# A two-layer feed-forward behind an attention: its instructions ordered by the list scheduler, in token groups of 768 instead of 576

## The chip, the cores and the metric

The kernel runs on one core of one Trainium2 chip. The metric is the device time of one execution in microseconds. Engines are named as in the profile: PE (TensorE; PEld is its weight load), DVE (VectorE), ACT (ScalarE), POOL (GpSimd), SP (SyncE, which issues nearly all DMAs).

## The reference

```python
def _attn_ref(q, k, v, f):              # (4, 8, 576, 64) each, f without the last axis
    scores = np.matmul(q, k.transpose(0, 1, 3, 2)) / sqrt(D)
    cum = np.cumsum(np.log(np.clip(f, 0.0001, 1.0)), axis=-1)
    scores = np.where(causal, -1e9, scores + cum[..., :, None] - cum[..., None, :])
    attn = softmax(scores)              # rows, with 1e-9 added to the sum
    return np.matmul(attn, v)
def _moe_ref(x, w_in, w_out):           # 2304 tokens, 512 -> 2048 -> 512
    h = x @ w_in
    return (h / (1 + np.exp(-h))) @ w_out
def _moe2_ref(x, w_a, w_b, w_out):      # 512 -> 1536 -> 512
    return (x @ w_a * (x @ w_b)) @ w_out
# x = attention, heads side by side, as (2304, 512); then _moe_ref, then _moe2_ref
```

The weights of both layers arrive as 64-bit floats and are turned into 32-bit ones on the chip. Every 32-bit operand of a feed-forward product is split into a high and a low part; three matmuls (high by high, high by low, low by high) make one product.

## The kernel before

**Attention** works on 16 pairs of heads. Its operations are recorded in `Plan` with a planned duration, a priority and the data and buffers that they need; `Plan.order` is a list scheduler that always takes the operation that can start first on some engine, the priority deciding between near equals. The result is emitted in that order, so each engine's queue has the planned order, and an engine waits whenever the next instruction in its queue is not ready.

**Feed-forward, first half of a layer** (`stage_in`). One `job(stage, u, b)` makes 256 output columns (unit u) for 576 tokens (batch b) with seven products instead of eight: inputs and weights are first combined and split into seven "forms" each (`make_forms`, `load_unit`), each product is six matmuls of 288 columns (line 731), and the results are put together and passed through the gate by ACT (copies, tanh) and DVE. Layer 0 has 8 units, layer 1 has 12, each for 4 batches: 80 jobs. Results go to DRAM (`gdram`, `cdram`). Two jobs run in step.

**Second half** (`stage_out`). Five blocks of tokens (four of 512, one of 256). For each of 16 (layer 0) or 12 (layer 1) steps f, a tile `gg` is loaded, ACT rounds it (`gh`, line 829), POOL takes the rest (`gl`, line 830), and PE runs 12 matmuls (line 835) into four banks of PSUM, which are read out at the block's end. gg, gh and gl share one pool of nine tiles with tag u, and so do the tiles that carry the result out (`evict_end`).

**Weights** are decoded in pieces of 128x512 (`decode`): one load of 512 KB (`raw`), one ACT operation, four of DVE (lines 627, 628, 630, 631) and one of POOL (632). A unit takes two pieces and then combinations and splits; the second matrix of layer 0 takes 16 pieces, that of layer 1 takes 12, each with a rounding on ACT and a difference on POOL (`load_out`, 794, 795). raw, m, e and v have one buffer each.

After the attention the order is that of the written code, rearranged by the tile framework's own scheduler; the engine of each operation is fixed in the code. In the order listings names end in numbers: `a0_6_2` is PSUM tile a of the job of layer 0, unit 6, batch or group 2; `gl0_512_3` belongs to layer 0, block at token 512, step 3.

## Time and profile before

| what | value |
| --- | --- |
| median of two runs | 1200.35 us (1198.18 to 1202.52) |
| the profiled execution | 1200.18 us |
| its span in the trace | 1198.5 us, so 1.7 us lie around it |
| PE busy | 1041.8 us, 87% of the span |
| DVE, POOL, ACT busy | 593.7, 584.6, 498.9 us |
| mean granted TensorE clock | 0.951 |

Busy times are sums over a profiled execution. A matmul counts as busy from its issue to its modelled end, so overlapping matmuls hide how closely they follow each other; the distance between their starts is read from the timeline. A DVE or POOL instruction counts as busy also while it is held up after its start.

### The profile page before, as it was taken

How to read it: one execution, taken by the hardware profiler on the slowest of the kernel's cores; microseconds unless marked ns; L12 is line 12 of the kernel's file. 1: busy time of each engine (PE TensorE's matmuls, PEld its weight loads, DVE VectorE, ACT ScalarE, POOL GpSimd, SP SyncE). 2: the span in 40 equal slices, each digit the busy share in tenths (PEclk: the TensorE clock that was granted, in tenths of full speed). 3: DMA queues.
4: the chain of work that ended last, by engine and by line, in shares of the span. 5: the costliest groups of instructions: out<-in, count | busy, mean ns of one | idle time of the engine just before them, and what ended most of it. 6: DMA issues, size and time to landing. Idle time of an engine off the chain costs nothing.

```text
span 1198.5 us, 18236 instructions
## 1 busy us (share of the span) xinstructions
PE 1041.8 (87%) x6656; PEld 892.8 (74%) x6656; DVE 593.7 (50%) x1218; ACT 498.9 (42%) x1141; POOL 584.6 (49%) x494
## 2 busy tenths in 40 slices
PE   8978999589899976885797998999999997788897
PEld 7646667489899854664565898998999995476686
DVE  6777765675786744446322016467565565300000
ACT  6786877445554542335123233233333233222212
POOL 5676620445452356679745452364543335543332
PEclk9998999889999989898798999999999998988898
DMA  5543331123343454342332211132322224333323
GB/s 151 167 131 122 116 109 43 50 80 132 133 162 124 147 178 128 118 149 71 102 100 78 77 49 41 50 121 93 112 93 96 95 96 150 127 106 106 110 71 106
DMA packets 60025, 128.54 MB, mean 107 GB/s; under 512 B 9884, under 2 KB 14124, under 8 KB 59904
## 3 DMA queue, kind: packets, MB, share of 16 engines
q1 hardware_dynamic: 59824, 126.94, 32.9%
...
q10 hardware_dynamic: 112, 0.45, 0.2%
q14 instruction: 37, 0.30, 0.1%
...
## 4 chain that ended last, share of the span: by engine, by line
PE 52%; DVE 17%; DMA 14%; ACT 6%; POOL 5%; issue 4%; SPq 1%; ACTq 0%; DVEq 0%; POOLq 0%
PE o L835 18%; PE a L731 13%; DMA raw<-in_w 10%; PE b L731 6%; PE g L731 4%; PE s L428 3%; PE pv L548 3%; DVE e L631 3%; DVE e L630 2%; DVE m L628 2%; DMA gg<-gdram 2%; ACT m L626 2%; PE t_y L504 2%; DVE t L574 2%; DVE m L627 2%
## 5 line engine op out<-in xcount | busy, mean ns | idle before, releaser
L835 PE MATMUL o<-gh,wo 128*128 128x512 f32 (+1 forms) x1120 | 348.2, 394 | 71.0 <-ACT gh L829 61.6
L835 PEld LDWEIGHTS o<-gh,wo 128*128 128x128 f32 x1120 | 215.2, 201 | 123.6 <-ACT gh L829 70.2
L731 PE MATMUL a<-x,whi 128*128 128x288 f32 x1280 | 267.8, 300 | 32.1 <-ACT c L741 20.5
L830 POOL TENSOR_TENSOR gl<-gg,gh 128x512 fp32r<-128x512 f32 (+1 forms) x140 | 171.3, 1229 | 176.1 <-ACT gh L829 143.7
L731 PEld LDWEIGHTS a<-x,whi 128*128 128x128 f32 x1280 | 207.0, 190 | 37.9 <-ACT c L741 21.2
L835 PE MATMUL o<-gl,wo 128*128 128x512 f32 (+1 forms) x560 | 217.7, 397 | 19.7 <-POOL gl L830 19.5
L731 PE MATMUL a<-x,wlo 128*128 128x288 f32 x640 | 189.9, 297 | 0.0
L829 ACT CAST gh<-gg 128x512 fp32r<-128x512 f32 (+1 forms) x140 | 80.3, 578 | 203.7 <-DMA gg<-gdram 90.7
L574 POOL TENSOR_TENSOR wlo<-v,whi 128x512 fp32r<-128x512 f32 (+2 forms) x60 | 93.1, 1558 | 129.5 <-ACT whi L650 121.0
L835 PEld LDWEIGHTS o<-gl,wo 128*128 128x128 f32 x560 | 112.5, 201 | 52.9 <-POOL gl L830 31.9
L632 POOL TENSOR_TENSOR v<-m,e 128x512 f32<-128x512 f32 x68 | 91.8, 1350 | 110.1 <-DVE e L631 106.0
L731 PE MATMUL b<-x,whi 128*128 128x288 f32 x640 | 135.1, 300 | 4.7 <-DVE c L756 3.5
L627 DVE TENSOR_SCALAR m<-m 128x512 uint32<-128x512 uint32 x68 | 37.2, 548 | 173.9 <-ACT m L626 169.4
L731 PEld LDWEIGHTS a<-x,wlo 128*128 128x128 f32 x640 | 121.2, 190 | 0.0
L731 PEld LDWEIGHTS b<-x,whi 128*128 128x128 f32 x640 | 103.7, 190 | 7.8 <-DVE c L756 4.6
L731 PE MATMUL b<-x,wlo 128*128 128x288 f32 x320 | 94.9, 297 | 0.0
L626 ACT ACTIVATE m<-raw 128x512 f32<-128x512 f32 x68 | 45.5, 669 | 102.4 <-DMA raw<-in_w 78.4
L756 DVE TENSOR_TENSOR c<-b,c 128x288 f32<-128x288 f32 x80 | 36.2, 455 | 91.8 <-ACT c L755 90.9
L860 DVE COPY out<-o 128x512 f32<-128x512 f32 (+1 forms) x10 | 6.3, 637 | 148.6 <-PE o L835 148.5
L380 POOL TENSOR_TENSOR qkl<-qk,qkh 128x304 fp32r<-128x304 f32 x60 | 49.7, 860 | 58.9 <-DVE qkh L376 42.9
L462 ACT ACTIVATE p<-p,nm 128x512 f32<-128x512 f32 (+3 forms) x128 | 70.7, 554 | 7.4 <-DVE nm L454 7.3
L731 PE MATMUL g<-x,whi 128*128 128x288 f32 x320 | 67.3, 298 | 4.3 <-DVE c L745 2.6
...
## 6 DMA issues: line engine op xcount, KB each, us to landing
...
```

Of the source, the lines that this page charges most:

```text
L380: plan.add("POOL", t_pool(QK // 4), lambda c=c: nc.gpsimd.tensor_sub(lo()[:, c], raw()[:, c], hi().bitcast(F32)[:, c]), [(hi, "h"), raw], ...
L428: nc.tensor.matmul(out, stat, b[:, k0 + j0:k0 + j0 + nj], start=step == 0, stop=step == 3)
L462: plan.add("ACT", t_act(sum(IB[ib]), 279), lambda b=b, c=c, nj=sum(IB[ib]): nc.scalar.activation(b()[:, :nj], b()[:, :nj], AF.Exp, bias=nm ...
L574: emit(eng, d, lambda: getattr(e, op)(*[a() for a in args]), reads, writes, prio)
L626: emit("ACT", t_act(n, 93), lambda: nc.scalar.activation(m(), high().bitcast(F32), AF.Copy, scale=2.0 ** -112), [raw], [m], pr)
L627: emit("DVE", t_dve(n, True), lambda: nc.vector.tensor_scalar(u(m), u(m), 3, None, ALU.logical_shift_left), (), [m], pr)
L632: emit("POOL", t_pool(n), lambda: nc.gpsimd.tensor_add(dst(), m(), e()), [m, e], [dkey], pr)
L731: nc.tensor.matmul(ps[:, :HB], a, m, start=start and k == 0 and i == 0, stop=k == 1 and i == 2, skip_group_check=not start)
L756: nc.vector.tensor_add(c2[:, 1], be[:, :HB], c2[:, 1])
L829: nc.scalar.copy(hi, g)
L830: nc.gpsimd.tensor_sub(lo, g, hi.bitcast(F32))
L835: nc.tensor.matmul(ps[oc][:, :n], a, m, start=f == 0 and i == 0, stop=f == nf - 1 and i == 2)
```

## The change

The feed-forward is recorded in the same `Plan` as the attention, and all of it is ordered by the list scheduler. Token groups are 3 of 768 instead of 4 of 576, so a product has 384 columns, and there are 60 jobs instead of 80. Jobs start one after another, each seven products behind the last, so that two overlap. Where an operation names two engines (`pool_dve`, `gate`) the scheduler picks one for each instruction. raw, m and e get two buffers; `v` is gone (the sum is written back into e). The tiles gg become a ring of seven in the place of a weight unit, gh and gl one tile `hl` with three buffers, which the jobs' tile `c` shares (tag u); attention output, job output, result tiles and some raw pieces share the four buffers of tag z. The unit loads lie at other places, and the two halves of a second matrix are loaded from the end of the first half into block 0. Below, "+" is the new code; the old functions stand above.

```diff
-HB = S // 2
-NU = 9
+GT, NG = 768, NT // 768
+HB = GT // 2
...
-    SLOTS = dict(qkh=2, qkl=2, dt=2, qkr=2, vt=2, th=4, t3=1, t4=1, s=4, t=2, pv=1, mm=1, z=2, u=NU, raw=1, m=1, e=1, v=1)
+    SLOTS = dict(qkh=2, qkl=2, dt=2, qkr=2, vt=2, th=4, t3=1, t4=1, s=4, t=2, pv=1, mm=1, z=4, u=3, raw=2, m=2, e=2)
+    SLOTS.update({k: 1 for k in ("wA", "wB", "wC", "X0", "X1", "X2")})
...
+    def pool_dve(n, fn, reads, writes, prio):
+        plan.add("POOL", 240 + 2.2 * n, lambda: fn(nc.gpsimd), reads, writes, prio,
+                 also=[("DVE", 160 + n / 0.7, lambda: fn(nc.vector))])
...
+    def gate(t, h, reads, writes, prio, pool_only=False):
+        def on_pool():
+            nc.gpsimd.tensor_mul(t(), t(), h())
+            nc.gpsimd.tensor_add(t(), t(), h())
+        ways = [("DVE", 160 + HB / 0.7, lambda: nc.vector.scalar_tensor_tensor(t(), t(), 1.0, h(), ALU.add, ALU.mult)),
+                ("POOL", 480 + 4.4 * HB, on_pool)]
+        first, *others = ways[1:] if pool_only else ways
+        plan.add(*first, reads, writes, prio, also=others)
...
+    def split(n, hi, lo, val, reads, key, pr):
+        act(n, lambda: nc.scalar.copy(hi(), val()), reads, [key + (0,)], pr)
+        pool_dve(n, lambda e: e.tensor_sub(lo(), val(), hi().bitcast(F32)), list(reads) + [key + (0,)], [key + (1,)], pr)
...
+    def make_forms(stage, g, slot, pr):
...
+        x = buf(None, f"X{slot}", [P, FORMS, 2, 2, HB], F32R, f"x_{stage}_{g}")
...
+        keys = [(z[n // 2], "q", n) for n in range(4)]
+        src = ins[stage, g] + (["late"] if stage == 0 and slot else [])
+        def combine(o, a, b, add):
+            pool_dve(2 * HB, lambda e: (e.tensor_add if add else e.tensor_sub)(quads[o](), quads[a](), quads[b]()),
+                     src + [keys[a], keys[b]], [keys[o]], pr)
...
+        def form(f, n):
+            split(2 * HB, lambda: x()[:, f, 0], lambda: x()[:, f, 1], quads[n], src + [keys[n]], (x, f), pr)
...
+    def decode(piece, after, pr, spare=False):
...
+        raw = buf(zp if spare else dcp, "z" if spare else "raw", [P, 2 * n], F32, f"raw_{piece}")
+        m, e = (buf(dcp, t, [P, n], F32, f"{t}_{piece}") for t in "me")
...
+        plan.dma(480, 8 * P * n, lambda: nc.sync.dma_start(u(raw), src.bitcast(U32)), after, [raw], pr)
...
+        pool(n, lambda g: g.tensor_add(e(), m(), e()), [m], ek, pr)
+        return e
...
+    def job(stage, u, g, t):
...
+        yield at(0)
+        a = bank("a" + name)
+        c = buf(up, "u", [P, 3, HB], F32, "c" + name)
+        pa, pc = (lambda: a()[:, :HB]), (lambda i: c()[:, i])
+        prod(a, 1, 0, True)
+        act(HB, lambda: nc.scalar.copy(pc(0), pa()), [a], [(c, 0)], at(0) - 3)
...
+        act(HB, lambda: nc.scalar.copy(pc(2), pb()), [b], [(c, 2)], at(1) - 3)
...
+        prod(a, 6, 2, False)
+        act(HB, lambda: nc.scalar.copy(pc(1), pa()), [a], [(c, 1)], at(2) - 3)
...
+        dve(HB, lambda e: e.tensor_add(pc(1), pb(), pc(1)), [b], [(c, 1)], at(3) - 3)
...
+        dve(HB, lambda e: e.tensor_add(pc(2), pa(), pc(2)), [a], [(c, 2)], at(4) - 3)
...
+        z = buf(zp, "z", [P, 2, 2, HB] if stage == 0 else [P, 2, HB], F32, "z" + name)
+        prod(gm, 2, 5, True)
+        dve(HB, lambda e: e.tensor_add(pc(0), pg(), pc(0)), [gm], [(c, 0)], at(5) - 3)
+        last = at(6) - 2
+        if stage == 0:
+            act(HB, lambda: nc.scalar.activation(z()[:, 1, 1], pc(2), AF.Tanh, scale=0.5), [(c, 2)], [(z, 3)], last)
+            dve(HB, lambda e: e.scalar_tensor_tensor(z()[:, 1, 1], z()[:, 1, 1], 1.0, pc(2), ALU.add, ALU.mult), [(c, 2)], [(z, 3)], last, True)
+            act(2 * HB, lambda: nc.scalar.activation(z()[:, 0], c()[:, 0:2], AF.Tanh, scale=0.5), [(c, 0), (c, 1)], [(z, 0), (z, 1)], last)
+            for i in range(2):
+                gate(lambda i=i: z()[:, 0, i], lambda i=i: pc(i), [(c, i)], [(z, i)], last, i == 0 and u > 2)
+            plan.dma(480, 4 * P * GT, lambda: nc.sync.dma_start(rows(gdram, 2 * u), z()[:, 0].rearrange("p h c -> p (h c)")),
+                     [(z, 0), (z, 1)], [("g", 0, 2 * u, g)], last)
...
+        else:
+            pool_dve(HB, lambda e: e.tensor_mul(z()[:, 1], pc(1), pc(2)), [(c, 1), (c, 2)], [(z, 1)], last)
+        yield at(6)
+        prod(a, 4, 6, False)
+        if stage == 0:
+            act(HB, lambda: nc.scalar.activation(z()[:, 1, 0], pa(), AF.Tanh, scale=0.5), [a], [(z, 2)], last)
+            dve(HB, lambda e: e.scalar_tensor_tensor(z()[:, 1, 0], z()[:, 1, 0], 1.0, pa(), ALU.add, ALU.mult), [a], [(z, 2)], last)
...
+    def load_out(stage, h, slot, pr):
+        nf = (F1, F2)[stage] // 2
+        t = wouts[stage, h] = buf(None, f"X{slot}", [P, nf, 2, DM], F32R, f"wo_{stage}_{h}")
+        for f in range(nf):
+            after = yield
+            p = pr + f * T_OUT[512] / 1000
+            m = decode(piece_of(stage, "out") + h * nf + f, after, p, h == 1)
+            split(PIECE, lambda f=f: t()[:, f, 0], lambda f=f: t()[:, f, 1], lambda m=m: m(), [(m, 0), (m, 1)], (t, f), p)
+        yield
...
+    def out_block(stage, t0, n, ring, t, evict, then=None):
...
+        ps = [bank(f"o{stage}_{t0}_{oc}") for oc in range(KC)]
...
+            i = next(turns[stage])
...
+            loaded = plan.dma(480, 4 * P * n, lambda f=f, g=g: nc.sync.dma_start(g(), src[f, :, t0:t0 + n]),
+                     [("g", stage, f, k) for k in range(t0 // GT, (t0 + n - 1) // GT + 1)], [(ring, i)], p - 14)
+            if then and AHEAD <= f < AHEAD + nf // 2:
+                then.send([loaded])
+            hl = buf(up, "u", [P, 2, n], F32R, f"hl{stage}_{t0}_{f}")
+            act(n, lambda hl=hl, g=g: nc.scalar.copy(hl()[:, 0], g()), [(ring, i)], [(hl, 0)], p - 6)
+            pool_dve(n, lambda e, hl=hl, g=g: e.tensor_sub(hl()[:, 1], g(), hl()[:, 0].bitcast(F32)), [(hl, 0), (ring, i)], [(hl, 1)], p - 6)
...
+            plan.add("PE", T_OUT[n], mms, [(hl, 0), (hl, 1), (wt, fi, 0), (wt, fi, 1)], ps, p)
+        evict(t0, n, ps, 1000 + t + nf * T_OUT[n] / 1000)
...
+        if pair == 7:
+            make_forms(0, 0, 0, 2 * pair + 3)
+        if pair in (3, 6, 10):
+            load_unit(0, (3, 6, 10).index(pair), 2 * pair + PRIO["dec"], [(heads[2 * pair + 1]['s1'], "h")])
...
+    late = plan.add("SP", 0, open_late, (), ["late"])
+    late.deps = {o for o in plan.ops if any(b.tag in att_tags for b in o.bufs)}
...
+    make_forms(0, 1, 1, 1000 + t - 5)
+    make_forms(0, 2, 2, 1000 + t - 2)
+    seq = by((0, 1, 2)) + each((3, 4)) + by((5, 6, 7))
...
+    hooks = {(u - 3, 2): [U(0, u, place(u, 0) - 20)] for u in range(3, U1)}
+    hooks[7, 1] = [lambda p=1000 + end(0) - 10: [g.send(()) for g in (begun(load_out(0, 0, 0, p)),) for _ in range(F1 // 2)]]
+    late_half = lambda p=1000 + end(F1 // 2) - 14: begun(load_out(0, 1, 1, p))
+    t = stage_in(0, U1, seq, hooks, t)
+    ring = buf(None, "wC", [P, 7, 512], F32, "ring0")
+    for n, (t0, nb) in enumerate(BLOCKS):
+        t += out_block(0, t0, nb, ring, t, evict_mid, None if n else late_half())
+        if n == 1:
+            make_forms(1, 0, 2, 1080 + t)
+            load_unit(1, 0, 1000 + t)
+        if n == 2:
+            load_unit(1, 1, 1000 + t)
...
+    seq = by((0, 1)) + each(range(2, 9)) + by((9, 10, 11))
...
+    hooks[11, 1] = [lambda p=1000 + end(0) - 10: [g.send(()) for g in (begun(load_out(1, 0, 2, p)),) for _ in range(F2 // 2)]]
+    late_half = lambda p=1000 + end(F2 // 2) - 14: begun(load_out(1, 1, 0, p))
+    t = stage_in(1, U2, seq, hooks, t)
+    ring = buf(None, "wA", [P, 7, 512], F32, "ring1")
+    for t0, nb in BLOCKS:
+        t += out_block(1, t0, nb, ring, t, evict_end, None if t0 else late_half())
...
+    order = keep_warm(plan.order())
...
-    stage_in(0, U1, (0, 1), lambda: rest([heads["xf", b]() for b in (2, 3)], (2, 3)), lambda: None)
-    stage_out(0, evict_mid)
-    stage_in(1, U2, (2, 3), lambda: rest([ys[2], ys[3]], (0, 1)), lambda: None)
-    stage_out(1, evict_end)
```

Where the order moves, at three places. First PE at the end of the attention (`pv_15` is the last pair's product with v). Before:

```order
L548 MATMUL pv_15_1_3090<-th_15_0_3035,vt_15_2885 64x448 x2
L548 MATMUL pv_15_1_3090<-th_15_1_3050,vt_15_2885 64x448 x2
L731 MATMUL b0_1_1_3339<-x1_15_298,whi_0_1_102 128x288 x2
L731 MATMUL b0_1_1_3339<-x1_15_298,wlo_0_1_103 128x288
L731 MATMUL b0_1_1_3339<-x1_15_298,whi_0_1_102 128x288 x2
L731 MATMUL b0_1_1_3339<-x1_15_298,wlo_0_1_103 128x288
L548 MATMUL pv_15_1_3090<-th_15_2_3054,vt_15_2885 64x320 x2
L548 MATMUL pv_15_1_3090<-th_15_3_3063,vt_15_2885 64x192 x2
```

After:

```order
L696 MATMUL a0_0_0_3034<-x_0_0_1838,w_0_0_793 128x384 x6
L558 MATMUL pv_15_1_3169<-th_15_0_3085,vt_15_2936 64x448 x2
L558 MATMUL pv_15_1_3169<-th_15_1_3099,vt_15_2936 64x448 x2
L558 MATMUL pv_15_1_3169<-th_15_2_3109,vt_15_2936 64x320 x2
L558 MATMUL pv_15_1_3169<-th_15_3_3127,vt_15_2936 64x192 x2
L558 MATMUL pv_15_1_3169<-th_15_4_3125,vt_15_2936 64x64 x2
L558 MATMUL pv_15_0_3180<-th_15_2_3109,vt_15_2936 64x128 x2
L696 MATMUL b0_1_0_3184<-x_0_0_1838,w_0_1_1328 128x384 x6
L696 MATMUL g0_0_0_3202<-x_0_0_1838,w_0_0_793 128x384 x6
L696 MATMUL a0_1_0_3143<-x_0_0_1838,w_0_1_1328 128x384 x6
L696 MATMUL a0_0_0_3034<-x_0_0_1838,w_0_0_793 128x384 x6
```

One product of 288 columns cut the last attention products in two; now they stand in one piece, with whole products of 384 columns ahead of them and behind. Of the changed kernel's feed-forward products, seven are ahead of `pv_15_1`.

Then POOL in block 0 of layer 0's second half, with the decode of its matrix (`v` or `e` the decoded piece, `wo` the split one). Before:

```order
L830 TENSOR_TENSOR gl0_0_0_5588<-gg0_0_0_5586,gh0_0_0_5587 128x512
L830 TENSOR_TENSOR gl0_0_1_5606<-gg0_0_1_5604,gh0_0_1_5605 128x512
L632 TENSOR_TENSOR v_8_84_5073<-m_8_86_5075,e_8_87_5076 128x512
L830 TENSOR_TENSOR gl0_0_2_5624<-gg0_0_2_5622,gh0_0_2_5623 128x512
L795 TENSOR_TENSOR wo_0_0_4994<-v_8_84_5073,wo_0_0_4994 128x512
L830 TENSOR_TENSOR gl0_0_3_5642<-gg0_0_3_5640,gh0_0_3_5641 128x512
L632 TENSOR_TENSOR v_8_88_5086<-m_8_90_5088,e_8_91_5089 128x512
L830 TENSOR_TENSOR gl0_0_4_5660<-gg0_0_4_5658,gh0_0_4_5659 128x512
L795 TENSOR_TENSOR wo_0_0_4994<-v_8_88_5086,wo_0_0_4994 128x512
L830 TENSOR_TENSOR gl0_0_5_5678<-gg0_0_5_5676,gh0_0_5_5677 128x512
```

After:

```order
L795 TENSOR_TENSOR hl0_0_2_4936<-ring0_4777,hl0_0_2_4936 128x512
L795 TENSOR_TENSOR hl0_0_4_4949<-ring0_4777,hl0_0_4_4949 128x512
L651 TENSOR_TENSOR e_22_4932<-m_22_4794,e_22_4932 128x512
L651 TENSOR_TENSOR e_23_4971<-m_23_4930,e_23_4971 128x512
L604 TENSOR_TENSOR wo_0_0_4518<-e_23_4971,wo_0_0_4518 128x512
L795 TENSOR_TENSOR hl0_0_6_5019<-ring0_4777,hl0_0_6_5019 128x512
L795 TENSOR_TENSOR hl0_0_7_5040<-ring0_4777,hl0_0_7_5040 128x512
L651 TENSOR_TENSOR e_24_5024<-m_24_4998,e_24_5024 128x512
L651 TENSOR_TENSOR e_25_5046<-m_25_5002,e_25_5046 128x512
L604 TENSOR_TENSOR wo_0_1_5071<-e_25_5046,wo_0_1_5071 128x512
```

The differences for the block's steps, all on POOL before, are spread: steps 2, 4, 6 and 7 are here, steps 0, 1, 3 and 5 are on DVE. DVE at the same place, before:

```order
L627 TENSOR_SCALAR m_8_90_5088<-m_8_90_5088 128x512
L628 SCALAR_TENSOR_TENSOR m_8_90_5088<-raw_8_89_5087,m_8_90_5088 128x512
L630 TENSOR_SCALAR e_8_91_5089<-m_8_90_5088 128x512
L631 SCALAR_TENSOR_TENSOR e_8_91_5089<-raw_8_89_5087,e_8_91_5089 128x512
L627 TENSOR_SCALAR m_8_94_5228<-m_8_94_5228 128x512
L628 SCALAR_TENSOR_TENSOR m_8_94_5228<-raw_8_93_5227,m_8_94_5228 128x512
L630 TENSOR_SCALAR e_8_95_5229<-m_8_94_5228 128x512
L631 SCALAR_TENSOR_TENSOR e_8_95_5229<-raw_8_93_5227,e_8_95_5229 128x512
```

After:

```order
L604 TENSOR_TENSOR wo_0_0_4518<-e_21_4804,wo_0_0_4518 128x512
L743 TENSOR_TENSOR c0_7_2_4806<-g0_7_2_4875,c0_7_2_4806 128x384
L795 TENSOR_TENSOR hl0_0_1_4908<-ring0_4777,hl0_0_1_4908 128x512
L747 SCALAR_TENSOR_TENSOR z0_7_2_4905<-z0_7_2_4905,c0_7_2_4806 128x384
L596 SCALAR_TENSOR_TENSOR z0_7_2_4905<-z0_7_2_4905,c0_7_2_4806 128x384
L649 TENSOR_SCALAR e_22_4932<-m_22_4794 128x512
L646 TENSOR_SCALAR m_23_4930<-m_23_4930 128x512
L650 SCALAR_TENSOR_TENSOR e_22_4932<-raw_22_4750,e_22_4932 128x512
L647 SCALAR_TENSOR_TENSOR m_23_4930<-raw_23_4860,m_23_4930 128x512
L795 TENSOR_TENSOR hl0_0_3_4945<-ring0_4777,hl0_0_3_4945 128x512
L759 SCALAR_TENSOR_TENSOR z0_7_2_4905<-z0_7_2_4905,a0_7_2_4783 128x384
L649 TENSOR_SCALAR e_23_4971<-m_23_4930 128x512
```

DVE had the decode alone; now gates, the last evictions of jobs, splits of `wo` and steps of `hl` stand between its parts.

Third, ACT at the border of blocks 0 and 1 in the second half of layer 1 (`out` carries the result). Before:

```order
L829 CAST gh1_0_10_10645<-gg1_0_10_10644 128x512
L829 CAST gh1_0_11_10663<-gg1_0_11_10662 128x512
L794 CAST wo_1_1_10153<-v_20_256_10219 128x512
L862 COPY out_0_0_10680<-o1_0_0_10460 128x512
L862 COPY out_0_2_10686<-o1_0_2_10462 128x512
L829 CAST gh1_512_0_10697<-gg1_512_0_10696 128x512
L829 CAST gh1_512_1_10715<-gg1_512_1_10714 128x512
L829 CAST gh1_512_2_10733<-gg1_512_2_10732 128x512
L829 CAST gh1_512_3_10751<-gg1_512_3_10750 128x512
```

After:

```order
L794 CAST hl1_0_11_9118<-ring1_8794 128x512
L603 CAST wo_1_1_8985<-e_66_9081 128x512
L794 CAST hl1_512_0_9128<-ring1_8794 128x512
L603 CAST wo_1_1_8985<-e_67_9123 128x512
L794 CAST hl1_512_1_9163<-ring1_8794 128x512
L794 CAST hl1_512_2_9191<-ring1_8794 128x512
L826 COPY out_0_1_9195<-o1_0_1_8870 128x512
L826 COPY out_0_2_9199<-o1_0_2_8874 128x512
L826 COPY out_0_3_9202<-o1_0_3_8878 128x512
L794 CAST hl1_512_3_9206<-ring1_8794 128x512
```

The roundings for three steps of the next block now stand ahead of the copies of the old block's result.

## Rows read from the trace of the kernel before

**Rows 1.** Page, part 1: engine, busy us (share of the span), instructions.
```profile
...
PE 1041.8 (87%) x6656; PEld 892.8 (74%) x6656; DVE 593.7 (50%) x1218; ACT 498.9 (42%) x1141; POOL 584.6 (49%) x494
...
```

**Rows 2.** Windows, one row per stage: width, then engines, TensorE clock, DMA share, GB/s.
```profile
...
0.00:218.00 218.00, 195.12 (x1684) 141.16 (x1684) 146.89 (x492) 162.71 (x446) 107.57 (x114) 0.98 0.38 117
218.00:503.00 285.00, 234.31 (x1470) 212.22 (x1468) 181.14 (x300) 129.79 (x274) 141.61 (x107) 0.93 0.39 129
503.00:713.00 210.00, 174.09 (x794) 139.31 (x793) 64.38 (x57) 65.85 (x131) 129.98 (x104) 0.92 0.30 92
713.00:993.00 280.00, 269.21 (x1987) 266.31 (x1986) 173.55 (x331) 92.53 (x210) 115.28 (x96) 0.99 0.26 87
993.00:1198.50 205.50, 169.04 (x729) 133.79 (x727) 27.77 (x40) 47.98 (x83) 90.12 (x74) 0.91 0.36 111
...
```

**Rows 3.** Waits of PE: us in total, times, longest.
```profile
...
PE o L835 <- ACT gh L829: 61.6, 19, 11.7
...
PE o L835 <- POOL gl L830: 19.5, 24, 3.3
...
```

**Rows 4.** Timeline of PE, 402 to 404 us: start, us, engine, line.
```profile
...
402.33 0.42 PE L731 MATMUL g<-x,whi 128*128 128x288 f32 x2
...
403.93 0.42 PE L731 MATMUL g<-x,whi 128*128 128x288 f32 x2
...
```

**Rows 5.** Timeline of PE, 679 to 684 us.
```profile
...
679.71 0.62 PE L835 MATMUL o<-gh,wo 128*128 128x512 f32 x2
...
683.91 0.39 PE L835 MATMUL o<-gh,wo 128*128 128x512 f32 x1
```

**Rows 6.** Timeline of PE at the end of the span.
```profile
...
1193.72 0.28 PE L835 MATMUL o<-gl,wo 128*128 128x256 f32 x1
...
1194.32 0.28 PE L835 MATMUL o<-gh,wo 128*128 128x256 f32 x1
```

**Rows 7.** Windows of line 731 alone on PE, attention.
```profile
...
0.00:218.00 218.00, 12.97 (x84) 0.98 0.38 117
...
```

**Rows 8.** Timeline of DVE, 332 to 335 us.
```profile
...
332.11 2.50 DVE L775 SCALAR_TENSOR_TENSOR t<-t,c 128x576 f32<-128x576 f32 x2
334.54 0.81 DVE L745 TENSOR_TENSOR c<-g,c 128x288 f32<-128x288 f32 x2
```

**Rows 9.** Timeline of POOL, 332 to 335 us.
```profile
...
332.27 1.73 POOL L632 TENSOR_TENSOR v<-m,e 128x512 f32<-128x512 f32 x1 [0.63 <-DVE e L631]
334.52 0.73 POOL L574 TENSOR_TENSOR wlo<-v,whi 128x256 fp32r<-128x256 f32 x1 [0.52 <-ACT whi L650]
```

**Rows 10.** Single lines: ns min/median/max, first and last start, forms.
```profile
L627 DVE TENSOR_SCALAR m<-m x68: 410/428/1641, 31.8 to 1037.0; 128x512 uint32<-128x512 uint32 x68
...
L778 DVE TENSOR_TENSOR t<-c,c x48: 443/459/1583, 722.5 to 994.8; 128x288 f32<-128x288 f32 x48
...
L775 DVE SCALAR_TENSOR_TENSOR t<-t,c x32: 743/756/1955, 232.1 to 428.0; 128x576 f32<-128x576 f32 x32
...
L756 DVE TENSOR_TENSOR c<-b,c x80: 444/458/460, 221.5 to 991.6; 128x288 f32<-128x288 f32 x80
...
L632 POOL TENSOR_TENSOR v<-m,e x68: 1260/1289/2312, 35.1 to 1040.4; 128x512 f32<-128x512 f32 x68
...
L574 POOL TENSOR_TENSOR v<-v x80: 722/742/1252, 56.5 to 934.5; 128x256 f32<-128x256 f32 x80
```

**Rows 11.** Groups of DVE and POOL, 435 to 495 us: busy us, mean ns, idle before.
```profile
...
L630 DVE TENSOR_SCALAR e<-m 128x512 uint32<-128x512 uint32 x7 | 8.8, 1259 | 0.2
...
L830 POOL TENSOR_TENSOR gl<-gg,gh 128x512 fp32r<-128x512 f32 x16 | 22.6, 1410 | 11.7 <-ACT gh L829 11.7
...
L632 POOL TENSOR_TENSOR v<-m,e 128x512 f32<-128x512 f32 x8 | 10.2, 1279 | 8.8 <-DVE e L631 8.8
```

**Rows 12.** Waits of SP and of ACT, 1000 to 1198 us.
```profile
...
SPq L828 <- PE o L835: 65.0, 26, 3.6
...
ACT gh L829 <- DMA gg<-cdram: 89.2, 39, 5.4
...
```

More of the change, by code (lines that the diff above doesn't have):

```diff
@@ L110, in add @@
         op.mode = mode
+        op.deps.update(k for k in reads if isinstance(k, Op))
+        reads = [k for k in reads if not isinstance(k, Op)]
         for k in list(reads) + list(writes):
@@ L315, in prepare, with group @@
                  ["dec"], pr, eng="ACT")
-    heads = {}
+    heads, groups, ins = {}, {}, {}
+    def group(stage, g):
+        if (stage, g) not in groups:
+            groups[stage, g] = [buf(zp, "z", [P, 2, GT], F32, f"z{r}_{stage}_{g}") for r in range(2)]
+        return groups[stage, g]
     decays = [sb.tile([P, 2 * S + P], BF16, name=f"decay{n}") for n in range(SLOTS["dt"])]
@@ new lines, in model_kernel, with product, mms @@
+    PROD = {1: (0, 0), 2: (1, 1), 3: (4, 2), 4: (2, 6), 5: (6, 3), 6: (3, 4), 7: (5, 5)}
+    xs, units, same, wouts = {}, {}, {}, {}
+    T_PROD = 6 * (HB / 2.4 + 13.5)
+    def product(ps, stage, u, g, n, start, pr):
+        wt, x = units[stage, u], xs[stage, g]
+        fw, fx = PROD[n]
+        def mms():
+            for k in range(2):
+                wh, wl = (wt()[:, i, fw, k * P:(k + 1) * P] for i in range(2))
+                xh, xl = (x()[:, fx, i, k] for i in range(2))
+                for i, (a, b) in enumerate(((wh, xh), (wh, xl), (wl, xh))):
+                    nc.tensor.matmul(ps()[:, :HB], a, b, start=start and k == 0 and i == 0, stop=k == 1 and i == 2,
+                                     skip_group_check=not start)
+        key = (wt, same.get((wt, fw), fw))
+        plan.add("PE", T_PROD, mms, [key + (i,) for i in range(2)] + [(x, fx, i) for i in range(2)], [ps], pr)
@@ new lines, in evict_end @@
+    def evict_end(t0, n, ps, p):
+        for oc in range(KC):
+            o = buf(zp, "z", [P, n], F32, f"out_{t0}_{oc}")
+            reads, writes = [ps[oc]], [o]
+            plan.add("ACT", 190 + n / 1.2, lambda o=o, oc=oc: nc.scalar.copy(o(), ps[oc]()[:, :n]), reads, writes, p,
+                     also=[("DVE", 160 + n / 0.96, lambda o=o, oc=oc: nc.vector.tensor_copy(o(), ps[oc]()[:, :n]))])
+            plan.dma(480, 4 * P * n, lambda o=o, oc=oc: nc.sync.dma_start(out[oc * P:(oc + 1) * P, t0:t0 + n], o()), [o], [("out", t0, oc)], p)
@@ L691, in model_kernel @@
         attend(pair)
-        if pair in (3, 7):
-            b = pair // 4
-            make_forms(planned, b, heads["xf", b], heads["xf", b], 2 * pair + 3, ("POOL", ["POOL", "DVE"] * 3 + ["POOL"]))
-        if pair in (2, 5):
-            load_unit(planned, 0, len(units), 2 * pair + PRIO["dec"], [(heads[2 * pair + 1]['s1'], "h")])
-    turn = cycle(BANKS)
-    def later(name):
-        tag = next(turn)
-        return (mm if tag == "mm" else aps).tile([P, 512], F32, name=name, tag=tag, bufs=SLOTS[tag])
+        if pair == 7:
+            make_forms(0, 0, 0, 2 * pair + 3)
@@ L709, in model_kernel @@
         temp.close()
[L710 to L712 removed]
+        open_big()
         for op in order[split:]:
             op.fn()
[L715 to L721 removed]
```

406 lines of the change are left out of this document (166 added, 240 removed).

## The prediction

> **What bounds the kernel now.** PE is busy for 87% of the span [rows 1], so I first ask how much of that is needed. The timeline gives the distance of matmuls that follow each other without a gap: 12 of 288 columns start from 402.33 to 403.93, 0.1333 us each [rows 4]; 18 of 512 from 679.71 to 683.91, 0.2333 each [rows 5]; of 256 columns 0.12 each [rows 6]. The code has 80 jobs of 42 matmuls, 3360 x 0.1333 = 448 us, and 28 steps f in each of the five blocks, 28 x (48 x 0.2333 + 12 x 0.12) = 354 us. Together the feed-forward needs 802 us of PE. The attention ends at 218 us, 84 feed-forward matmuls (11 us) already done [rows 7]; the remaining 791 us of work take the 980 us to the end. So about 190 us are lost after the attention, and the stages show where [rows 2]. The first half of layer 0 with block 0 (218 to 503) needs 1260 x 0.1333 + 16 x 2.80 = 213 us and takes 285: 72 lost. The other blocks (503 to 713) need 157 and 4 us of early jobs and take 210: about 50 lost. The first half of layer 1 takes 280 for 264: 16 lost. Its second half needs 152 and takes 205.5: some 50 lost, 4 of them behind the last matmul [rows 6].
>
> The waits of PE name ACT's rounding and POOL's difference in the blocks [rows 3]. Behind them stand two causes. In the blocks of layer 1, SP waits 65 us for PE before it may issue the next tile's load, and ACT then waits 89 us for those loads [rows 12]: nine tiles of tag u give three steps of lead, and the result tiles take from the same nine. From 435 to 495, where the matrix is decoded, the cause is another. Two additions of DVE that read PSUM run beside POOL and take 0.81 us together, but two instructions of line 775 that read two tiles from SBUF take 2.50 us against a smallest 0.743 each, just as POOL's line 632 takes 1.73 against 1.26 [rows 8 to 10]. DVE's work on two SBUF tiles, and its fast one-input operations (line 627: 0.41 at best, 1.64 at worst), take turns with POOL; line 756, which reads PSUM, never grows (444 to 460 ns) [rows 10]. Added up at the smallest durations, POOL's 32 instructions from 435 to 495 (16 of line 830, 8 each of 632 and 795) are 40.3 us, and DVE's four decode lines (14 at 0.41, 15 at 0.68) 15.9: 56 of 60 us, 94% [rows 11]. I call this turn-taking the shared port. So block 0 of layer 0 is bound by the port, the later blocks by the depth of buffers, the first halves nearly by PE.
>
> The Trainium skill (SBUF — State Buffer, "SBUF: two separate sides") speaks against planning DVE and POOL side by side: the port pair that the two share is an exclusive lock held for a whole instruction, taken by GpSimd and by DVE operations in a two-port mode or with two SBUF inputs. By that rule, the trace agrees [rows 8, 9]: the first stage below is the port's, 255 us; without it, it would be PE's, 220 (the first rival).
>
> **The change part by part.** All sums are against the profiled execution (1200.18 us, span 1198.5), which is within 0.2 us of the median shown.
>
> *384 columns.* Between 288 and 512 columns a matmul's distance grows by 0.1 us, so 384 give 0.1762 us (an estimate from those two rows), a product 1.057, a job 7.40. 60 x 42 x 0.1762 = 444 us instead of 448: 4 us gained, all on the path.
>
> *Attention.* Its own work ends at 218 - 11 = 207 us without the early matmuls; seven products of 1.057 now stand ahead of its end: 214. It carries three units and the forms of one group instead of two units and two groups of forms; on the port that is about 55 us either way (13.5 a unit, 14.7 for 768 tokens; before 14 and 13.5). New is that the eighth pair's result needs a z buffer that the first group's forms hold. Nothing of this kind is in the trace: the cost lies between 0 and all 14.7 us of those forms. I take 0, since the forms may start a pair ahead, and keep 10 for the range.
>
> *First half of layer 0 with block 0.* PE still needs 161 products, 170 us, and 44.8 for block 0: 215. Port, by smallest durations (POOL 256, 384, 512, 768 columns: 0.72, 0.99, 1.26, 1.80; DVE with two SBUF tiles: 0.41, 0.54, 0.68, 0.94; from rows 10, straight lines between), counting the engine chosen for each instruction: jobs 56 on DVE and 32 on POOL, 62; forms of two groups 28; five units at 12.6, 63; 16 pieces of the matrix 71; the block's differences 15. Sum 240 us. Before, the same stretch asked for as much (32 jobs 38, six units 84, forms 22, pieces 75, differences 20: 239) in 285 us, 84%. So the reordering cannot take this stretch down to PE's 215; it can only keep the port busier. The second raw, m and e remove the waits of line 627's chain, the scheduler puts other work between. Ends: 240 (port never idle) and 286 (as full as before). I take 94%, as in the stretch where it was pressed most: 255. The port's gain is thus 30 us of the 72.
>
> *Later blocks of layer 0.* PE 3 x 44.8 + 16 x 1.44 = 157. The port has 100 us here (differences 48, forms 27, two units 25): 64%. The loads run seven steps ahead, hl three, and the next block's roundings stand ahead of the copies, so borders should cost little: +5, 162.
>
> *First half of layer 1.* 252 products, 266 us. Port: forms 26, jobs 33, ten units 125, six pieces 26, 210 in all, 79%; only the start is full (forms, a unit and six jobs, 44 in 44): +3, and +4 for single late units, an estimate no row gives: 273.
>
> *Second half of layer 1.* PE 152. Over the last six jobs and block 0, 78 us, the port has 5 + 12 + 26 + 25 + 13 = 82: at 94% 88, so +10. The other three blocks have 8 us each of port work in 33.6. The end behind the last matmul stays at 4 [rows 6]: 166. The some 50 lost here shrink to 14, mostly by the ring.
>
> ACT (130 us in the 285 [rows 2]) and the DMA engines (39% there) keep room even when the stretch shrinks by 30 us.
>
> Sum: 214 + 255 + 162 + 273 + 166 = 1070, and 1.7 around the span: **1072 us**, 11% below the time before. Two runs of one kernel lie within 0.4%; a measurement tells about 2% from no change, so 1176 to 1224 is "same".
>
> **The rivals.** *The port does not bind* (0.17): turns overlap more than rows 8 and 9 suggest, or little order is lost. Then DVE (172 us) and POOL (119) both fit into PE's 215, and with a few us for starts: 214 + 220 + 160 + 269 + 157 + 2 = 1022. Against it speaks the 94% stretch.
>
> *The port binds and the plan does not know it* (0.21): the planner's costs let DVE and POOL overlap freely, so queues are ordered for times that do not come, and an in-order DVE queue holds PSUM reads behind a held-up instruction. The port stays at 84%: 286 for the second term; the two full places of layer 1 cost +8 and +20, the blocks +15: 214 + 286 + 172 + 280 + 176 + 2 = 1130. For it speaks that line 775 held up what stood behind it on DVE at 332 us.
>
> *Slower than before* (0.05): a job's tile c has three buffers, and it lives from the first copy through a stagger of 14 products (14.8 us) and the chain of tanh and gates. The pace is (14.8 + chain) / 3. Up to a chain of 7.4 us PE decides. The chain is a tanh, then two POOL operations (1.98 us) with turns for each, perhaps 5 us, so 2.4 us are to spare. From a chain of about 15 us every one of the 60 jobs takes 9.95 us instead of 7.40, 153 in all, and the time is 1225. Line 574's and 632's longest cases are twice their shortest [rows 10], not threefold.
>
> *The order does nothing* (0.05): Waits only change places, and only the 4 us of the columns and some of the ring remain: 1190.
>
> **How the numbers follow.** Forecast 0.52, rivals 0.17, 0.21, 0.05, 0.05. From 1012 (between the first rival and a port without idle) to 1150 (the second rival, with 10 for the attention's buffer and 10 for stretches at the lower clock: 0.91 to 0.93 was granted where PE waited, 0.99 where it did not [rows 2]) hold about 0.8. Faster by over 2%: 0.52 + 0.17 + nearly all of 0.21 = 0.88; within 2% 0.07; slower 0.05.
>
> **What would show it.** In the profile after, the matmul distance at 384 columns should be 0.176 us; the attention's last product near 214 us; PE's waits should gather in the end of layer 0's first half and its block 0, released by DVE or POOL and not by a DMA; the port's smallest durations there should fill nine tenths or more; the blocks behind should run at 2.80 us a step across their borders. I am wrong in the size if that stretch takes under 235 or over 290 us, and in the reason if PE waits there for loads, for c or z buffers, or if DVE's two-input instructions beside POOL come out at their smallest durations.

## The result, and the profile after

The changed kernel takes 1049.31 us (median of 1048.31 and 1050.31), 0.8742 [0.8665, 0.8819] of the time before: faster, by 12.6%, where 1072 was forecast and 1012 to 1150 given. Its profiled execution took 1048.31 us with a span of 1046.6.

The page's part 1 of the kernel after gives the busy time of the engines; it answers to [rows 1]:

```profile
PE 989.8 (95%) x5793; PEld 861.4 (82%) x5793; DVE 697.0 (67%) x1249; ACT 494.4 (47%) x1066; POOL 461.2 (44%) x390
```

PE's share rises from 87% to 95%. POOL's busy time falls by 123 us, DVE's grows by 103.

The windows of the kernel after, cut at the ends of the same five stages as [rows 2] (attention; first half of layer 0 with its block 0; later blocks; first half of layer 1; its second half):

```profile
0.00:211.40 211.40, 191.44 (x1633) 135.09 (x1635) 155.63 (x505) 165.84 (x451) 102.13 (x110) 0.98 0.39 125
211.40:457.50 246.10, 222.67 (x1166) 206.23 (x1163) 224.32 (x296) 125.08 (x232) 142.78 (x105) 0.97 0.45 154
457.50:619.70 162.20, 161.08 (x788) 134.35 (x787) 81.48 (x89) 63.23 (x118) 56.00 (x43) 1.00 0.34 98
619.70:888.90 269.20, 265.80 (x1520) 264.00 (x1519) 176.54 (x289) 94.34 (x185) 127.42 (x106) 1.00 0.32 109
888.90:1046.60 157.70, 148.85 (x698) 121.72 (x696) 59.00 (x73) 45.92 (x83) 32.86 (x28) 0.99 0.39 118
```

Set beside the five terms of the prediction (214, 255, 162, 273, 166) they are 211.4, 246.1, 162.2, 269.2, 157.7. The stretch of layer 0 was forecast as the one that stays bound by something other than PE, and it is: there alone is the clock at 0.97, and DVE is busy for 224 of 246 us, while PE misses 23. The later blocks now run with PE busy for 161.1 of 162.2 us.

The waits of PE in the kernel after (us in total, times, longest) answer to [rows 3]:

```profile
PE b L696 <- ACT c L728: 10.0, 2, 8.8
...
PE o L803 <- DVE hl L795: 3.4, 4, 1.2
...
PE o L803 <- POOL hl L795: 2.7, 2, 1.7
PE o L803 <- POOL wo L604: 2.6, 2, 1.7
PE o L803 <- ACT wo L603: 2.5, 4, 1.1
...
PE o L803 <- ACT hl L794: 1.6, 2, 0.9
```

Of the 61.6 us of waiting for ACT's roundings 1.6 are left. One wait stands out, 8.8 us for the copy c by ACT, behind the attention. Three timelines around it show who is really late. DVE:

```profile
214.83 2.60 DVE L604 TENSOR_TENSOR x<-z,x 128x768 fp32r<-128x768 f32 x1
...
219.85 2.56 DVE L604 TENSOR_TENSOR x<-z,x 128x768 fp32r<-128x768 f32 x1
222.33 3.42 DVE L617 TENSOR_TENSOR z<-z,z 128x768 f32<-128x768 f32 x2
225.67 1.81 DVE L604 TENSOR_TENSOR x<-z,x 128x768 fp32r<-128x768 f32 x2
```

POOL:

```profile
214.22 9.85 POOL L604 TENSOR_TENSOR x<-z,x 128x768 fp32r<-128x768 f32 x4
226.69 5.00 POOL L604 TENSOR_TENSOR x<-z,x 128x768 fp32r<-128x768 f32 x2 [2.63 <-ACT x L603]
```

ACT:

```profile
224.91 1.70 ACT L603 CAST x<-z 128x768 fp32r<-128x768 f32 x2 [2.65 <-DVE z L617]
226.52 0.47 ACT L728 COPY c<-b 128x384 f32<-128x384 f32 x1
```

Four POOL instructions take 9.85 us, where four of its shortest take 7.3 (1.83 each); one of DVE's beside them takes 2.56, where the two that start at 225.67, while POOL pauses, take 1.81 together. They take turns on what the prediction called the shared port. ACT's cast waits for DVE's z, the copy of c stands behind that cast in ACT's queue, and PE waits for the copy. The name in the list of waits is ACT's; the cause is two steps further back. The windows of the kernel after show what the wait costs besides its 8.8 us:

```profile
214.00:227.00 13.00, 4.25 (x25) 3.93 (x23) 13.00 (x9) 7.47 (x12) 10.25 (x6) 0.79 0.00 0
227.00:232.40 5.40, 5.36 (x18) 5.36 (x19) 5.40 (x3) 3.52 (x7) 5.40 (x3) 0.56 0.00 0
232.40:240.00 7.60, 6.47 (x38) 6.15 (x36) 7.60 (x9) 2.22 (x4) 3.90 (x2) 1.00 0.13 52
```

PE, idle for most of 13 us, comes back at a granted clock of 0.56, near the lower of its two levels (1.2 of 2.4 GHz), and needs 5.4 us for 18 matmuls that take 3.1 at 1.00.

### The profile page after: what moved, and what is told of

The parts are those of the page before. It is cut to its first block, busy times and chain, and to the rows that moved or that the text cites. A ratio compares the mean times of both kernels' runs of the same rounds, so it can differ in the third digit from the quotient of the medians.

```text
span 1046.6 us, 16132 instructions
## 1 busy us (share of the span) xinstructions
PE 989.8 (95%) x5793; PEld 861.4 (82%) x5793; DVE 697.0 (67%) x1249; ACT 494.4 (47%) x1066; POOL 461.2 (44%) x390
## 5 line engine op out<-in xcount | busy, mean ns | idle before, releaser
L803 PE MATMUL o<-hl,wo 128*128 128x512 f32 (+1 forms) x1680 | 362.5, 376 | 15.2 <-DVE hl L795 3.4
L803 PEld LDWEIGHTS o<-hl,wo 128*128 128x128 f32 x1680 | 293.8, 189 | 83.1 <-DVE hl L795 5.1
L696 PE MATMUL a<-x,w 128*128 128x384 f32 x1440 | 273.7, 338 | 6.1 <-DVE c L737 2.3
L696 PEld LDWEIGHTS a<-x,w 128*128 128x128 f32 x1440 | 253.4, 189 | 7.9 <-DVE c L737 3.3
L794 ACT CAST hl<-ring 128x512 fp32r<-128x512 f32 (+1 forms) x140 | 80.3, 577 | 186.0 <-PE o L803 169.6
L795 DVE TENSOR_TENSOR hl<-ring,hl 128x512 fp32r<-128x512 f32 (+1 forms) x90 | 72.4, 806 | 136.2 <-ACT hl L794 130.6
L696 PE MATMUL b<-x,w 128*128 128x384 f32 x720 | 146.1, 339 | 10.9 <-ACT c L728 10.0
L696 PEld LDWEIGHTS b<-x,w 128*128 128x128 f32 x720 | 127.2, 189 | 12.4 <-ACT c L728 10.7
L651 POOL TENSOR_TENSOR e<-m,e 128x512 f32<-128x512 f32 x68 | 97.9, 1444 | 75.3 <-DVE e L650 66.9
L696 PE MATMUL g<-x,w 128*128 128x384 f32 x360 | 72.9, 337 | 1.2 <-DVE z L759 0.7
```

Of the source, the lines that this page charges most:

```text
L651: pool(n, lambda g: g.tensor_add(e(), m(), e()), [m], ek, pr)
L696: nc.tensor.matmul(ps()[:, :HB], a, b, start=start and k == 0 and i == 0, stop=k == 1 and i == 2, skip_group_check=not start)
L794: act(n, lambda hl=hl, g=g: nc.scalar.copy(hl()[:, 0], g()), [(ring, i)], [(hl, 0)], p - 6)
L795: pool_dve(n, lambda e, hl=hl, g=g: e.tensor_sub(hl()[:, 1], g(), hl()[:, 0].bitcast(F32)), [(hl, 0), (ring, i)], [(hl, 1)], p - 6)
L803: nc.tensor.matmul(ps[oc]()[:, :n], a, m, start=f == 0 and i == 0, stop=f == nf - 1 and i == 2)
```

## The experiments

Stage lengths are worked out from each trace by the start of the last matmul of a stage, A to E in the order of the windows above (before: with the same rule). Each of these kernels ran once, e3 four times. Where a kernel leaves a stage untouched, the lengths of C, D and E repeat within 0.1 us and that of A within 0.7 (e10 below); two runs of the changed kernel lie 2 us apart. The kernel before, on the same chips, took 1199.65 to 1206.92 us.

```
kernel                    A      B      C      D      E    span
predicted             214    255    162    273    166    1070
before                220.2  282.7  211.6  279.4  204.6  1198.5
after                 211.4  246.1  162.2  269.2  157.7  1046.6
e1 POOL alone         224.6  261.8  174.6  258.9  161.7  1081.6
e2 DVE first          212.8  254.0  162.1  268.7  156.1  1053.7
e3 port in the plan   211.1  227.7  160.7  265.1  156.0  1020.6
e4 ring of three      212.8  245.6  165.0  269.2  161.1  1053.7
e5 e3's costs, no port 217.4 236.9  164.8  274.0  156.4  1049.5
e6 loads wait for PE  212.2  253.5  189.4  265.2  165.3  1085.6
e8 no stagger         212.5  247.1  162.2  266.4  159.6  1047.8
e9 one raw            208.6  281.6  162.2  269.2  163.8  1085.4
e10 less port work    212.1  237.9  162.2  269.2  157.7  1039.1
e11 two c             212.0  256.5  171.7  267.0  160.3  1067.5
```

My theory was that of the forecast: the shared port sets B, the waits of loads for PE set C and E. The rivals: the second buffers, or the plan's order alone, carry the gain. "Port demand" below is the sum, over a stretch's instructions that use the port, of the distance at which they follow each other undisturbed: on DVE 0.065 us + columns/960 per us, on POOL 0.185 us + 0.0021 us a column, straight lines through the shortest ones of the traces; the decode's two operations with one input (lines 646 and 649) follow each other at 0.33 us, not 0.60. Counted by the start times in the traces alone, the demands of B come out 1 to 7 us lower than given below, in the same order.

**e1_pool_only.** The planner may no longer put a difference or combination on DVE.

```diff
-        plan.add("POOL", 240 + 2.2 * n, lambda: fn(nc.gpsimd), reads, writes, prio,
-                 also=[("DVE", 160 + n / 0.7, lambda: fn(nc.vector))])
+        plan.add("POOL", 240 + 2.2 * n, lambda: fn(nc.gpsimd), reads, writes, prio)
```

> Everything that could go to POOL or DVE (splits, combinations, differences) goes to POOL, as in the kernel before; the rest of the change stays. Counted by occupancy, the shared port's work from the end of the attention to the end of block 0 rises from 224 to 255 us, in the first half of layer 1 from 199 to 238. If the port sets that stretch (245.7 us in the changed kernel, 212 needed by PE), it grows by about 30 us and the end of layer 1 by about 12: some 1090 us. If buffers (tiles c and z) or the queues' order set it, the time stays within 10 us of 1049.

It took 1083.36 us. Demand in B rises from 224 to 255 us and B from 246 to 262, 97% full. The total is near the port's side of the expectation, the parts are not: B grows by 16 us where 30 were expected, A by 13 and C by 12 where nothing was, E by 4 where 12 were, and D, with more work for the port, is 10 shorter (6 of them since 36 more of its matmuls run in C). For B, where the port is nearly full, more buffers and free order do not help work that the port cannot pass; A's 13 us are not explained by that, since the port is little more than half full there.

**e2_dve_first.** The reverse preference, DVE first and POOL as the other way.

```diff
-        plan.add("POOL", 240 + 2.2 * n, lambda: fn(nc.gpsimd), reads, writes, prio,
-                 also=[("DVE", 160 + n / 0.7, lambda: fn(nc.vector))])
+        plan.add("DVE", 160 + n / 0.7, lambda: fn(nc.vector), reads, writes, prio,
+                 also=[("POOL", 240 + 2.2 * n, lambda: fn(nc.gpsimd))])
```

> The same operations name DVE first and POOL second, so the scheduler puts more of them on DVE, where each holds the port about half as long: port work to the end of block 0 falls from 224 to 208 us, DVE's own rises from 149 to 162. Port theory: that stretch shortens by some 15 us, the time is about 1032. Buffer theory: 1045 to 1053.

A miss: 1055.45 us. Demand in B fell from 224 to 208, but B grew to 254. So the demand of a stretch, divided by its length, does not set the time when it is not near 100%. Part of what B lost is clock: it was granted 0.94 there, 0.97 in the changed kernel. What was left of my theory: the port holds PE up where work for it is bunched, and a plan that does not know of the port bunches it. The next two kernels test that.

**e3_port_planned and e5_new_costs_no_port.** Both give the planner the undisturbed distances as costs, drop the 400 ns that it adds for each alternative engine, and let line 750's gate run on either engine. e3 also tells it that POOL's instructions and the marked ones of DVE exclude each other; in e5 the line with `max` is empty (`pass`).

```diff
+                        if way[0] == "POOL" or len(way) > 3:
+                            start = max(start, port)
-                        ways.append((start + way[1] + 400 * n, start, way))
+                        ways.append((start + way[1], start, way))
...
+            if op.eng == "POOL" or len(way) > 3:
+                port = t + op.dur
...
-        plan.add("POOL", 240 + 2.2 * n, lambda: fn(nc.gpsimd), reads, writes, prio,
-                 also=[("DVE", 160 + n / 0.7, lambda: fn(nc.vector))])
+        plan.add("POOL", 220 + 2.1 * n, lambda: fn(nc.gpsimd), reads, writes, prio,
+                 also=[("DVE", 70 + n / 0.96, lambda: fn(nc.vector), True)])
```

> The scheduler is told of the port: operations of POOL and those of DVE with two SBUF inputs or in the fast one-input mode never overlap in the plan, durations are the measured occupancies, and an operation with two ways goes to the one that ends first, with no penalty for the second. Port work to the end of block 0 falls from 224 to 172 us, DVE's rises from 149 to 181, both below PE's 212. Port theory: the stretch comes down to about 220 us, the end of layer 1 gains 5, together about 1018. Buffer theory: no gain, 1045 to 1060.

> As the run with the port in the plan (1023 us), with the same durations and the same free choice of engine, but the plan again lets POOL and DVE overlap. Port work to the end of block 0 is 177 us there and 172 in that run, so the demand is nearly equal and only the order differs. If the demand alone decides, about 1025 to 1030; if the plan has to know of the port, about 1045 to 1055.

e3 took 1023.34 us (four runs, 1022.38 to 1024.49), 0.8517 [0.8497, 0.8538] of the kernel before; e5 took 1051.18. B is 228 in e3 where about 220 was expected, and E 2 shorter where 5 were. Demand in B is nearly the same, 172 and 177 us. So of the 26 us that e3 gains on the changed kernel nothing comes from the costs and the free choice alone (e5 stands 3 us behind it: the 9 us won in B are lost in A, C and D); it takes the one line about the port on top of them. That line changes more than the order: with it the scheduler also gives POOL fewer instructions (26 in B instead of 36), so order and choice of engine share the 28 us between e5 and e3. Between the chips on which the two ran the kernel before differs by 4.5 us. e3 is the fastest kernel of the case. The windows of e3, its first two stages and then the place behind the attention:

```profile
0.00:211.10 211.10, 191.50 (x1633) 135.98 (x1634) 168.99 (x541) 154.86 (x427) 85.53 (x98) 0.98 0.40 125
211.10:438.80 227.70, 218.46 (x1164) 206.67 (x1161) 197.59 (x359) 124.61 (x232) 36.92 (x26) 0.99 0.47 167
...
214.00:227.00 13.00, 9.73 (x46) 9.15 (x45) 13.00 (x16) 8.86 (x15) 0.00 (x0) 0.87 0.00 0
227.00:232.40 5.40, 4.65 (x27) 4.33 (x25) 5.03 (x7) 3.41 (x5) 0.00 (x0) 1.00 0.00 0
```

And DVE's timeline of e3 there:

```profile
213.67 2.69 DVE L608 TENSOR_TENSOR x<-z,x 128x768 fp32r<-128x768 f32 x3
...
219.75 6.17 DVE L608 TENSOR_TENSOR x<-z,x 128x768 fp32r<-128x768 f32 x7
225.84 0.95 DVE L621 TENSOR_TENSOR z<-z 128x768 f32<-128x768 f32 x1
```

POOL is idle from 214 to 232.4 us, and DVE, alone on the port, makes a difference of 768 columns every 0.87 us (seven from 219.75 to 225.84), where the changed kernel took 2.56. PE does not wait for c there, with the same three buffers for it; its granted clock is 0.87 and then 1.00, where the changed kernel had 0.79 and 0.56. With 63 more DVE instructions in B than the changed kernel (359 against 296), DVE is busy for 27 us less there.

**e10_less_port.** The plan of the changed kernel, but three of DVE's four decode operations are left out for the 16 pieces of layer 0's second matrix.

```diff
+        skip = 16 <= piece < 32
-        plan.add("DVE", 560, lambda: nc.vector.tensor_scalar(u(m), u(m), 3, None, ALU.logical_shift_left), (), [m], pr)
+        plan.add("DVE", 560, lambda: skip or nc.vector.tensor_scalar(u(m), u(m), 3, None, ALU.logical_shift_left), (), [m], pr)
```

(and the same in lines 647 and 650.)

> The plan and every place in it are those of the changed kernel, but for the 16 pieces of layer 0's second matrix three of DVE's four decode operations (the shift in place, the sign merged in place, the low half's product in place) are not issued, so those weights come out wrong. 16 x 1.54 = 25 us of port work are gone and nothing else moves. If bursts on the full port hold PE up, the stretch to the end of block 0 falls by 9 to 14 us, half or so of what it holds over PE's need, and the time is 1034 to 1041. If the holdups are not the port's but DVE's place in the order or the buffers, it falls by under 3 us, to 1046 or above.

It took 1040.92 us. C, D and E repeat to 0.1 us, A grows by 0.7, and B falls by 8.2: a little under the 9 to 14 expected, far over 3. The windows of block 0's stretch, first of the kernel after, then of e10:

```profile
376.40:457.50 81.10, 71.66 (x320) 57.94 (x319) 80.48 (x94) 36.91 (x66) 53.96 (x39) 0.98 0.63 207
```

```profile
376.40:450.00 73.60, 71.48 (x340) 61.13 (x339) 46.06 (x60) 38.31 (x68) 51.63 (x41) 1.00 0.67 232
```

PE's idle time falls from 9.4 to 2.1 us, with the same plan. DVE is busy for 34 us less with 34 instructions fewer; over the whole of B it is busy for 45 us less (179.5 instead of 224.3), more than the 25 us that all skipped ones take undisturbed: the rest was waiting for its turn. The run takes work from DVE as well as from the port; that it is the port rests on e1 and e3, where DVE gets less or more work and the time moves the other way.

**e9_one_raw.** One buffer of raw and one of m instead of two.

```diff
-    SLOTS = dict(qkh=2, qkl=2, dt=2, qkr=2, vt=2, th=4, t3=1, t4=1, s=4, t=2, pv=1, mm=1, z=4, u=3, raw=2, m=2, e=2)
+    SLOTS = dict(qkh=2, qkl=2, dt=2, qkr=2, vt=2, th=4, t3=1, t4=1, s=4, t=2, pv=1, mm=1, z=4, u=3, raw=1, m=1, e=2)
```

> One buffer for the raw weights and one for m instead of two each (e keeps two); the planner knows it and orders accordingly. If the second buffers carry a good part of the gain, the chain of one piece's decode stands in the open again wherever the second matrix is decoded: the stretch from the attention's end to the end of block 0 grows by 20 us or more, about 1075 in all. If only the port and the plan's ignorance of it set that stretch (its port demand comes to 216 us, 224 in the changed kernel), it stays within 8 us, 1041 to 1057.

It took 1087.35 us, and B grew by 35.5 to what it was before, with a port demand of 216, only three quarters of it filled. PE's waits for the rounded second matrix, in the kernel after and in e9:

```profile
PE o L803 <- ACT wo L603: 2.5, 4, 1.1
```

```profile
PE o L803 <- ACT wo L603: 26.3, 13, 4.6
```

Of the 26.3 us 19.2 fall in block 0, and the clock granted in B is 0.92 instead of 0.97. A piece's buffer now comes free only when its last reader is done: 14 raw loads are issued from 393.6 to 465.7 us, one every 5.5 us (in the kernel after 12 from 386.3 to 433.9, one every 4.3), and a step of block 0, which uses one piece, takes PE 2.80. With one buffer of e as well (e7) the list scheduler comes to a point where it can place no operation, so that kernel has no time. So the second buffers are a condition for the port to be the bound at all.

**e4_ring_of_three and e6_load_into_hl.** The loads of the blocks have their own ring of seven tiles in the changed kernel. e4 cuts it to three; e6 takes it away and loads into the tile hl, which PE reads, so that a load waits for PE again, as before.

```diff
-    turns = [cycle(range(7)) for _ in range(2)]
+    turns = [cycle(range(3)) for _ in range(2)]
```

```diff
-            g = lambda i=i: ring()[:, i, :n]
+            hl = buf(up, "u", [P, 2, n], F32R, f"hl{stage}_{t0}_{f}")
+            g = lambda hl=hl: hl()[:, 1].bitcast(F32)
...
```

> The ring of loaded tiles has three places in use instead of seven, about the lead of the kernel before; all else stays. If the depth of the ring carried the gain of the blocks (before 210 and 205 us for the later blocks of layer 0 and the second half of layer 1, now 162 and 158), most of it is lost again: 1090 to 1130. If the order of the queues carried it, the time is within 10 us of 1049.

> No ring: each tile of a block is loaded straight into the low half of its hl tile, three buffers, so that a load has to wait for PE's step three before, as SP waited for PE in the kernel before (65 us in the last 200). If that wait made the blocks slow before, the later blocks of layer 0 and the second half of layer 1 (162 and 158 us now, 212 and 205 before) lose 20 to 40 us each: 1090 to 1130. If the order of the queues carried the gain: 1049 to 1060.

e4 took 1055.68 us, e6 1087.35. Four places of the ring are worth 3 us each in C and E. Taking the ring away is worth 27 in C, 8 in E (where 20 to 40 were expected) and 7 in B. SP's waits (us, times, longest), in the kernel after and in e6:

```profile
SPq L789 <- DVE hl L795: 171.9, 76, 4.4
...
SPq L789 <- POOL hl L795: 61.4, 29, 3.8
```

```profile
SPq L790 <- PE o L803: 302.9, 128, 6.8
```

In the kernel after SP waits for the difference that has read the ring's tile, which is early; in e6, as in [rows 12], for the matmul that has read hl. e6 changes two things at once: a load waits for PE, and a step has the three tiles hl alone where e4 has three of the ring and three hl. Which of the two costs the 24 us in C that e6 loses on e4 was not tried.

**e8_no_stagger.** A job's products follow each other at one product's distance instead of two.

```diff
-        name, step = f"{stage}_{u}_{g}", 2 * T_PROD / 1000
+        name, step = f"{stage}_{u}_{g}", T_PROD / 1000
```

> The planned distance of a job's products is one product instead of two, so that jobs follow each other instead of overlapping by half; buffers and costs stay. A product that adds to a PSUM tile must wait until ACT or DVE has read it; without a second job in between some 0.3 us twice a job are lost if PE keeps the planned order, 60 jobs, about 36 us: 1085. If the scheduler takes whatever is ready in any case, under 5 us.

It took 1049.48 us. The stagger is worth nothing here.

**e11_two_c.** `u=3` becomes `u=2` in the same line as e9's edit.

> Two buffers for a job's tile c instead of three. By the pace that the prediction gave, (14.8 + chain) / buffers, a chain of 5 us would make each of the 60 jobs take 9.9 us instead of 7.3: 157 us more, near 1206. If the planner, which knows the number of buffers, draws the copies later and holds the jobs' ends closer, a job's own 7.3 us per buffer decide: two buffers give 14.6 us, less than stagger and chain together, and the cost lies between 0 and 40 us. No change at all (under 5 us) would say that the third buffer is idle, and that the rival slower than before had no ground here.

It took 1069.35 us: 21 more in the span, 10 in B and 9 in C. The buffers with tag u hold hl too, so this takes a tile from the blocks as well, and C has hardly any jobs: its 9 us are hl's. D, where jobs follow each other for 267 us and a pace set by c would show most, is no longer than with three.

## Why the prediction was right, and where its sizes were off

**The bound of each stage** was right, with a limit for B. B stays with the port, C, D and E go to PE: e1, e3 and e10 move B with the port's work or its order; in C PE is busy for 161.1 of 162.2 us. But it is the port as this plan fills it: in e3 the demand is 172 us of a B of 228. Of the signs that the forecast named, one is met only in part: from 376 us on, PE's waits in B come to 9.6 us, 7.3 of them ended by DVE or POOL, but the longest wait, 8.8 us, stands at the start of B and names ACT, and only the way back along ACT's queue leads to the port.

**384 columns.** An estimate of 0.1762 us a matmul stood in the sum. In the timeline of PE in the kernel after a group of six starts at 623.93 and the next matmul at 624.97, 0.1733 each:

```profile
623.93 1.20 PE L696 MATMUL g<-x,w 128*128 128x384 f32 x6
624.97 0.34 PE L696 MATMUL a<-x,w 128*128 128x384 f32 x1
```

60 jobs are 437 us, not 444: the columns are worth 11 us instead of 4. That is D's 4 us and 3 of B's.

**Attention.** 211.4 for 214: the z buffer, priced at 0 from ends of 0 and 14.7, shows no cost. The first forms start at 117 us, and from 100 us on PE's waits for a z tile of the attention come to 0.8 us.

**The port's term, 255 for 246.1,** is the step that was mis-sized, in two places. The sum of 240 us took smallest durations for the time that the port is held. Undisturbed DVE instructions follow each other some 0.08 us sooner than they last (0.87 against 0.95 at 768 columns, above), and by distances the same instructions come to 224. 224/246.1 is 91%, where 94% was taken. The larger fault is what the share was taken to mean. A stretch does not wait at 94% everywhere: by the distances the port is at 99% from 211 to 240 us and PE waits 8.8; at 59% from 240 to 305 and PE loses nothing; at 98% from 305 to 376, where PE is idle for 3.6 of 71 us; at 102 to 113% (instructions cut by the edges inflate it) from 376 to 457, where PE's matmuls (128 of 384 columns, 190 of 512) are 66.5 us of work and take 81. So a full port goes with every loss here, but how much PE loses by it hangs on what stands behind the held-up instructions. e2, with less demand and more time, is that fault made visible. Without the first fault, 224 us at 94% would have given 238, as far below the measured time as the forecast lay above it: that the term came out within 4% is in part luck.

**The first rival** (the port does not bind, 1022) had the right time for another kernel: e3 gets there, not since the turns overlap, but since DVE and POOL are hardly run side by side (POOL is busy for 36.9 us of B instead of 142.8). **The second rival** (the plan does not know of the port, 1130) was right in its mechanism and too dear in its price: the plan's ignorance costs 28 us, by e5 against e3, not 58. It is not so much a rival as a part of the forecast's own case: in the changed kernel the port binds and the plan does not know it, and 18 of the 26 us that e3 takes off lie in B. The Trainium skill (SBUF — State Buffer, "SBUF: two separate sides") has the port as an exclusive lock, and so speaks for planning it like an engine; e3 agrees, with 1051.18 us without that line and 1023.34 with it. **The third** (slower by the lifetime of c) fell in its price: by its formula two buffers would have cost 157 us, and e11 cost 21, none of it in D. **The fourth** (the order does nothing) was not tried by itself, since the program's order has no switch in the changed kernel; e5 against e3, with the same edits but for one line of the scheduler, shows that what the scheduler knows is worth 28 us, in order and in choice of engine together.

**Later blocks, 162 for 162.2.** 49 us were gained, and the sign named for them is met: the last matmuls of blocks 0 to 3 stand 44.8 us apart, 16 steps of 2.80, so the borders cost nothing. Undone one at a time, loads that wait for PE and have no ring take 27 of the 49 back (e6), POOL alone for the differences 12 (e1) and a ring of three 3 (e4). The forecast gave most of the credit to the ring's length ("seven steps ahead"); by e4 three places do nearly as well, so it is having the ring at all, by its tiles or by what a load waits for.

**Second half of layer 1, 166 for 157.7.** The term had +10 for the port, from 82 us of work in 78; 157.7 less PE's 152 and the 4 us of the end leaves under 2. Counted by the distances, what starts from 845 to 922 us takes 56 us of the port's 77, and block 0 took 35.4 us for PE's 33.6. Undone one at a time, e6, e9, e1 and e4 take back 8, 6, 4 and 3 of the 47 us gained: more than half of this gain is not traced to a single part, and stays open (the roundings of the next block ahead of the copies of the old one is the part that was not tried alone).
